# Spectral layer and two expert layers: four frequencies kept inside SBUF, and decode steps moved between stages

## The chip, the cores and the metric

The program runs on one core of a Trainium2 chip. The metric is the device time of one execution in microseconds; a median of several executions is compared. TensorE (PE) does the matmuls, VectorE (DVE) and ScalarE (ACT) do elementwise work, GpSimd (POOL) some of it, and SyncE (SP) issues most transfers.

## The reference

Three layers follow each other on 2 x 3008 tokens of width 256.

```python
X = np.fft.rfft(x, axis=1)                       # x: (2, 3008, 256)
Yr = Xr @ w_r - Xi @ w_i + b_r
Yi = Xr @ w_i + Xi @ w_r + b_i
Yr = np.sign(Yr) * np.maximum(np.abs(Yr) - 0.01, 0.0)    # Yi likewise
y = np.fft.irfft(Yr + 1j * Yi, n=3008, axis=1)
h = x @ w_in                                     # first expert: (6016, 256) @ (256, 2048)
x = (h - np.tanh(h)) @ w_out
h = x @ w_in2                                    # second expert
out = (h * np.clip(h + 3.0, 0.0, 6.0) / 6.0) @ w_out2
```

The experts' weights arrive as float64.

## The kernel before

**The spectral layer.** The transform of length 3008 = 47 x 64 is done in two steps. `dft_a` is the first step: it takes one of 16 chunks of x (eight of each batch row), multiplies it by `amt` and leaves 24 complex frequencies k for both parities on 96 partitions. `dft_a_out` evicts the two PSUM banks of a chunk on ScalarE, back into the chunk's own buffer (`xa` for the first batch, `xb` for the second), and stores it from ScalarE's queue to the DRAM array `s1`. `load_bi` reads four frequencies at a time back from `s1` into `bi_all`, now with 128 partitions in another order. `dft_b(j)` is the second step for two frequencies: four matmuls (L301), which need `bi_all` and the matching part of `bmt`. `evict_b_hi`, `_lo` and `_neg` split its result into a high part `fh` and a low part `fl`. `linear(j)` is the complex matrix product in 24 matmuls. `shrink`, `shrink_hi`, `shrink_lo` apply bias and threshold and split again (`sh`, `sl`). `dft_c` and `dft_d` are the two steps of the inverse transform, with a store to DRAM between them (`co`).

The frequency loop runs over t = 0 to 23. Iteration t does `linear(t)`, `dft_c(t-2)`, `dft_b(t+2)`, and, while chunks of the second batch are left, one `dft_a`. Every engine executes its instructions in the order in which the code is written.

**The decode.** `w_steps` is a generator that turns one float64 weight chunk of 512 KB (`raw`) into high and low float32 parts. Each call of `w_step` emits its next piece: on ScalarE L172 and L173 or the rounding copy L182, on VectorE L175, L185, L190, L197, or a pair of L201 to L205. Five calls decode a chunk of an output matrix and seven a chunk of an input matrix, with four and eight VectorE instructions. One of the pieces issues the next load of a `raw` buffer; there are three. `ptr["dec"]` counts decoded chunks; the first expert has 16, and the loop decodes up to `NDEC` = 13 of them, four calls in each iteration from t = 2 on.

**The experts.** Tokens come in eight blocks of 752; a pass k = 0 to 7 takes one block through the first expert, a pass 8 to 15 one through the second. Each pass has eight groups g of hidden units. A group is seven products in PSUM banks `al`, `be` and `ga` (a fast 2 x 2 matrix scheme), the nonlinearity (`e`, `g`, `c`, `su`, `s`), its split (`gh`, `gl`), and the output matmuls. `first_group` is the first group of pass 0; its pieces stand between the last iterations' `dft_c`. `super_hook` is called at the positions a to e of each group and adds what is due there: operands of the next block, and decode steps. In pass 0 it calls `w_step` at all five positions of groups 1 to 7, in the later ones of the first expert at b, c and d of groups 1 to 5.

**Transfers.** The transfers of SyncE and ScalarE share eight semaphores (DMAHW0 to 7) in rotation. A transfer that reuses one is issued only when the one before it on that semaphore has landed.

The lines that the prediction names: L269 `dft_a`, L279 its eviction, L280 its store, L290 `load_bi`, L301 `dft_b`, L308 the high part `fh`, L315 the low part `fl`, L407 a difference of operands, L418 the high half of an operand, L538 the first eviction of `first_group`, L575, L587 and L596 evictions and sums of a group.

Of the kernel before, what the change touches and what calls it, by code (L numbers as in the profile page):

```python
# [10 lines left out]
F32 = mybir.dt.float32  # L11
# [9 lines left out]
K1 = 24  # L21
D = 256
# [5 lines left out]
def dft_constants():  # L28
# [44 lines left out]

    am96 = np.zeros((96, 96))
    am96[0:94] = am.reshape(94, 96)
    cm = cm.reshape(128, K1 * 128).astype(f)
# [11 lines left out]
def spectral_moe_kernel(ctx: ExitStack, tc: tile.TileContext, x, w_r, w_i, b_r, b_i,  # L88
# [48 lines left out]

    NDEC, NST = 13, 2
    w_src = {"1i": w1i, "1o": w1o, "2i": w2i, "2o": w2o}
# [72 lines left out]
    def w_step():  # L212
        next(w_gen, None)
# [20 lines left out]
    bias = ca.tile([128, 1, D], F32, name="bias")  # L234
    amt = ca.tile([96, 96], F32, name="amt")
    x1 = [wia.tile([128, 4, D], F32, tag=f"wo{5 + r}", name=f"xb{r}") for r in range(3)]
# [3 lines left out]
    wa = wa_cm.__enter__()  # L240
    x0 = [wa.tile([128, 4, D], F32, name=f"xa{r}") for r in range(8)]
    stores = []

    def load_x(i):
        if i >= 16:
            return
        b, c = divmod(i, 8)
        if b == 0:
            v = x.rearrange("b s d -> (b s) d")[0:96 * 32].rearrange("(r j) d -> r j d", j=32)
            sp.dma_start(out=x0[c][0:96], in_=v[:, 4 * c:4 * c + 4, :])  # L250
        else:
            v = x[b].rearrange("(r j) d -> r j d", j=32)[:, 4 * c:4 * c + 4, :]
            for r0, r1 in ((0, 80), (80, 94)):
                sp.dma_start(out=x1[c % 3][r0:r1], in_=v[r0:r1])
# [6 lines left out]
    def dft_a(i, finish=True):  # L261
        b, c = divmod(i, 8)
        xt = (x1[c % 3] if b else x0[c])[0:96]
        banks_ = []
        for g in range(2):
            p = bank("acc" if i < 8 and i % 2 else "h")
            pv = p[0:96].rearrange("p (u d) -> p u d", d=D)
            for u in range(2):
                pe.matmul(out=pv[:, u, :], lhsT=amt, rhs=xt[:, 2 * g + u, :], start=True, stop=True)  # L269
            banks_.append(pv)  # L270
        if finish:
            dft_a_out(i, banks_)
        return banks_

    def dft_a_out(i, banks_):
        b, c = divmod(i, 8)
        xt = (x1[c % 3] if b else x0[c])[0:96]
        for g in range(2):
            act.activation(out=xt[:, 2 * g:2 * g + 2, :], in_=banks_[g], func=ACTF.Copy)  # L279
        act.dma_start(out=s1w[b][:, 4 * c:4 * c + 4, :], in_=xt)  # L280

# [3 lines left out]
    def load_bi(i):  # L285
        if i >= 2 * K1 // GB:
            return
        b, g = divmod(i, K1 // GB)
        t = bi_ring[i % 3]
        sp.dma_start(out=t, in_=s1[b][g * GB:(g + 1) * GB].rearrange("k p d -> p k d"))  # L290
        bi_t[i] = t
# [316 lines left out]
    with tc.manual_schedule():  # L608
# [13 lines left out]
        for i in range(8):  # L622
            load_x(i)
        for r in range(3):
            pool.memset(x1[r][64:96], 0.0)
# [6 lines left out]
        load_bm(0)  # L632
        sp.dma_start(out=dmt, in_=dm)
        for k, w in enumerate((b_r, b_i)):
            sp.dma_start(out=bias[64 * k:64 * k + 64, 0, :],
                         in_=w.rearrange("(o d) -> o d", o=1).broadcast_to([64, D]))
        for i in range(8):
            dft_a(i)
        load_x(8)
        load_bi(0)  # L640
        load_x(9)
        load_bi(1)
        load_bm(1)
        load_cm(0, x0[7][0:1, 3, 0:1])
        load_x(10)
        w_load()
        wa_cm.__exit__(None, None, None)
        wpool["r"] = ctx.enter_context(tc.tile_pool(name="wr", bufs=1, side="right", reuse_waits="tile"))
        for k in range(2):
            split(lwH[:, k], lwL[:, k], lws[k])  # L650
        for j in range(2):
            dft_b(j)
            evict_b_hi(j)
            evict_b_lo(j)
            evict_b_neg(j)
        load_bi(2)
        NP = K1
        a_next = 8
        for t in range(NP):
# [10 lines left out]
            shrink(t)  # L670
            shrink_hi(t)
            if t + 2 < NP:
                evict_b_lo(t + 2)
            if t == NP - 1:
                first = first_group()
                next(first)
            if t + 2 < NP:
                evict_b_neg(t + 2)
            for _ in range(2):
                if t > 1 and ptr["dec"] < NDEC:  # L680
                    w_step()
# [11 lines left out]
            if t % 2 == 0:  # L693
                load_bm(t // 2 + 2)
                load_cm(t // 2 + 1, s_t[t][0].bitcast(F32)[0:1, 0, 0:1])
            if t > 0:
                load_x(10 + t)
            if t in (0, 1):
                w_load()
            if t % 2 == 1:  # L700
                load_bi((t + 1) // 2 + 2)
            for _ in range(NST):
                if t > 1 and ptr["dec"] < NDEC:
                    w_step()
# [10 lines left out]
            if t == 22:  # L715
                op_sub(T3, B22, B12)
                op_sub(T4, B21, T2)

# [14 lines left out]
        def super_hook(k, g, pos):  # L733
# [12 lines left out]
            if n < 2 * NS:  # L746
# [21 lines left out]
                if g == 7 and pos == "e":  # L768
                    op_split(n, "b22")
            if 1 <= g < 6 or k == 0 and g > 0:  # L770
                if (pos in "bcd" or k == 0) and k < NS:
                    w_step()
            if pos == "e" and k in (NS - 1, NS):
# [54 lines left out]
```

## Time and profile before

| | us |
|---|---|
| median of 3 runs (lowest, highest) | 1226.78 (1226.3, 1228.44) |
| profiled execution | 1225.78 |
| its span, first to last instruction | 1224.0 |
| TensorE busy | 1183.5 |
| VectorE busy | 962.5 |
| ScalarE busy | 880.8 |

The profile is of one execution. What lies between span and time is start and end of the program. Busy times overlap; a stage is read from its own rows. Where the granted clock of TensorE has no record yet, at the start, the column shows 1.00.

### The profile page before, as it was taken

To read this page: it belongs to the slowest core of one execution; us is meant where nothing else is said; L and a number is where in the kernel's file an instruction comes from. 1 tells how busy PE (TensorE), PEld (TensorE's weight loads), DVE (VectorE), ACT (ScalarE), POOL (GpSimd) and SP (SyncE) were. 2 spreads that over 40 slices of the span, in tenths; PEclk is the share of its full clock that TensorE was granted. 3 is DMA by queue.
4 is the path that set the end of the run, shared out by engine and by line. 5 is a ranking of instruction groups with operands and counts; after the bars stand their busy time and mean duration, and the time that the engine had idled before them with its cause. 6 is when DMAs were issued, how large, how long until landed. Compare 5 with 4: busy or idle time off the path is not lost.

```text
span 1224.0 us, 20880 instructions
## 1 busy us (share of the span) xinstructions
PE 1183.5 (97%) x7824; PEld 1163.0 (95%) x7824; DVE 962.5 (79%) x1808; ACT 880.8 (72%) x1836; POOL 158.7 (13%) x164
## 2 busy tenths in 40 slices
PE   5899979899999999999999999999999999999998
PEld 3799969899999999999999999999999999999998
DVE  0479988888888888888778787878787878787875
ACT  3477767777787777777777777777777777777775
POOL 1000010201102020202021320202020202020200
PEclk9899989999999999999999999999999999999999
DMA  9896522232212122211104530101010101001000
GB/s 269 239 334 209 185 86 67 99 106 74 74 49 98 66 69 69 61 60 44 43 1 166 185 130 1 51 1 52 1 52 1 52 1 35 18 22 31 10 18 26
DMA packets 47797, 96.51 MB, mean 79 GB/s; under 512 B 4448, under 2 KB 27488, under 8 KB 47696
## 3 DMA queue, kind: packets, MB, share of 16 engines
q1 hardware_dynamic: 41728, 74.08, 18.8%
q0 software_dynamic: 4032, 14.68, 3.9%
q10 hardware_dynamic: 1936, 6.42, 1.4%
q8 instruction: 61, 1.00, 0.3%
q14 instruction: 40, 0.33, 0.1%
HBM read 58.73 MB, written 36.44 MB: 78 GB/s over the span
## 4 chain that ended last, share of the span: by engine, by line
PE 76%; DVE 10%; ACT 10%; issue 3%; DMA 2%; SPq 0%; ACTq 0%; DVEq 0%
PE acc L119 13%; PE acc L121 13%; PE acc L120 13%; PE al L119 7%; PE al L120 6%; PE al L121 6%; PE be L121 3%; PE be L120 3%; PE be L119 3%; ACT gh L115 2%; DVE g L440 2%; PE ga L398 2%; PE ga L120 2%; PE ga L121 2%; PE ga L119 1%
## 5 line engine op out<-in xcount | busy, mean ns | idle before, releaser
L116 DVE TENSOR_TENSOR gl<-g,gh 128x376 fp32r<-128x376 f32 x509 | 290.4, 571 | 149.7 <-ACT gh L115 122.1
L115 ACT ACTIVATE gh<-g 128x376 fp32r<-128x376 f32 x509 | 263.5, 518 | 185.5 <-DVE g L443 91.8
L121 PE MATMUL acc<-wo,gl 128*128 128x256 f32 (+1 forms) x768 | 215.9, 281 | 0.0
L120 PE MATMUL acc<-wo,gh 128*128 128x256 f32 (+1 forms) x768 | 215.8, 281 | 0.0
L119 PE MATMUL acc<-wo,gh 128*128 128x256 f32 (+1 forms) x768 | 215.7, 281 | 0.0
L119 PE MATMUL acc<-gh,wo 128*128 128x376 f32 x512 | 173.2, 338 | 0.0
L121 PE MATMUL acc<-gh,wo 128*128 128x376 f32 x512 | 171.0, 334 | 0.0
L120 PE MATMUL acc<-gl,wo 128*128 128x376 f32 x512 | 170.7, 333 | 0.0
L120 PEld LDWEIGHTS acc<-wo,gh 128*128 128x128 f32 (+1 forms) x768 | 143.0, 186 | 0.0
L121 PEld LDWEIGHTS acc<-wo,gl 128*128 128x128 f32 (+1 forms) x768 | 143.0, 186 | 0.0
L119 PEld LDWEIGHTS acc<-wo,gh 128*128 128x128 f32 (+1 forms) x768 | 142.8, 186 | 0.0
L407 POOL TENSOR_TENSOR bmt<-bmt 128x376 f32<-128x376 f32 x62 | 73.9, 1192 | 521.5 <-ACT bmt L400 396.8
L443 DVE SCALAR_TENSOR_TENSOR g<-e,c 128x376 f32<-128x376 f32 x192 | 119.3, 621 | 12.5 <-ACT e L442 7.9
L442 ACT ACTIVATE e<-c,three 128x376 f32<-128x376 f32 x192 | 116.7, 608 | 8.0 <-DVE c L589 7.2
L440 DVE TENSOR_TENSOR g<-c,e 128x376 f32<-128x376 f32 x189 | 113.9, 603 | 8.2 <-ACT e L439 6.0
L423 POOL TENSOR_TENSOR cmL<-bmt,cmH 128x376 fp32r<-128x376 f32 x60 | 66.1, 1102 | 325.8 <-ACT cmH L418 322.5
L439 ACT ACTIVATE e<-c 128x376 f32<-128x376 f32 x189 | 97.5, 516 | 7.9 <-DVE c L589 7.7
L119 PEld LDWEIGHTS acc<-gh,wo 128*128 128x128 f32 x512 | 96.4, 188 | 0.0
L120 PEld LDWEIGHTS acc<-gl,wo 128*128 128x128 f32 x512 | 96.3, 188 | 0.0
L121 PEld LDWEIGHTS acc<-gh,wo 128*128 128x128 f32 x512 | 96.1, 188 | 0.0
L119 PE MATMUL al<-cmH,wi 128*128 128x376 f32 x256 | 87.8, 343 | 6.3 <-ACT bi_all L538 2.9
L579 ACT ACTIVATE s<-be 128x376 f32<-128x376 f32 x127 | 61.9, 487 | 39.8 <-PE be L121 39.4
(164 smaller groups left out, 2830.8 us busy)
## 6 DMA issues: line engine op xcount, KB each, us to landing
raw<-in_moe_w_in_dram SPq DMA_DIRECT2D x16, 512.0 KB, 5.0
raw<-in_moe_w_out_dram SPq DMA_DIRECT2D x16, 512.0 KB, 4.4
w2id<-wout SPq DMA_DIRECT2D x8, 896.0 KB, 4.3
wi<-w2id POOLq DMA_DIRECT2D x8, 896.0 KB, 4.9
bi_all<-s SPq DMA_DIRECT2D x12, 512.0 KB, 6.5
y1d<-y SPq DMA_DIRECT2D x32, 188.0 KB, 2.0
bmt<-y1d SPq DMA_DIRECT2D x8, 752.0 KB, 4.9
s<-co SPq DMA_DIRECT2D x23, 256.0 KB, 5.5
```

The source lines that it names most:

```text
L115: act.activation(out=hi, in_=src, func=ACTF.Copy)
L116: (lo_eng or dve).tensor_tensor(out=lo, in0=src, in1=hi.bitcast(F32), op=ALU.subtract)
L119: pe.matmul(out=out_ap, lhsT=lh, rhs=rh, start=start, stop=False, **kw)
L120: pe.matmul(out=out_ap, lhsT=lh, rhs=rl, start=False, stop=False, **kw)
L121: pe.matmul(out=out_ap, lhsT=ll, rhs=rh, start=False, stop=stop, **kw)
L407: eng.tensor_tensor(out=out, in0=a, in1=b, op=ALU.subtract)
L423: (eng or dve).tensor_tensor(out=l, in0=OPS[nm][0], in1=h.bitcast(F32), op=ALU.subtract)
L439: act.activation(out=e, in_=src, func=ACTF.Tanh)
L440: dve.tensor_tensor(out=g, in0=src, in1=e, op=ALU.subtract)
L442: act.activation(out=e, in_=src, func=ACTF.Relu, bias=three)
L443: dve.scalar_tensor_tensor(out=g, in0=e, scalar=6.0, in1=src, op0=ALU.min, op1=ALU.mult)
L579: act.activation(out=s5, in_=be, func=ACTF.Copy)
```

## The change

`am` gets 32 more columns, copies of those of frequencies 0 to 7, so that `dft_a` of the first batch leaves them on partitions 96 to 127 as well. The eight buffers `xa` become one tile. After chunk 7, four transfers from `xa` to `bi_all` replace the first `load_bi`. ScalarE and VectorE evict one bank each for the first nine chunks. The ninth chunk is transformed ahead of the loop. Four matmuls on zeros stand ahead of everything on TensorE.

The decode starts ahead of the loop with five calls. An iteration makes six calls up to t = 9 and three or four from t = 10 on. In pass 0 there are four calls in groups 1 to 5 until 16 chunks are decoded, and none in groups 6 and 7; in later passes position a of groups 1, 3 and 5 is added. Two differences of operands (T3, T4) go from GpSimd to VectorE, and the last `shrink_hi` stands behind the first part of `first_group`.

```diff
-    am96 = np.zeros((96, 96))
-    am96[0:94] = am.reshape(94, 96)
+    am96 = np.zeros((96, 128))
+    am96[0:94, 0:96] = am.reshape(94, 96)
+    am96[0:94, 96:128] = am.reshape(94, K1, 4)[:, 0:8].transpose(0, 2, 1).reshape(94, 32)
...
-    x0 = [wa.tile([128, 4, D], F32, name=f"xa{r}") for r in range(8)]
+    xa = wa.tile([128, 32, D], F32, name="xa")
+    x0 = [xa[:, 4 * r:4 * r + 4, :] for r in range(8)]
...
         for g in range(2):
-            act.activation(out=xt[:, 2 * g:2 * g + 2, :], in_=banks_[g], func=ACTF.Copy)
-        act.dma_start(out=s1w[b][:, 4 * c:4 * c + 4, :], in_=xt)
+            if g and i < A0:
+                dve.tensor_copy(out=xt[:, 2 * g:2 * g + 2, :], in_=banks_[g])
+            else:
+                act.activation(out=xt[:, 2 * g:2 * g + 2, :], in_=banks_[g], func=ACTF.Copy)
+        act.dma_start(out=s1w[b][:, 4 * c:4 * c + 4, :], in_=xt[0:96])
...
+        warm = ca.tile([128, 256], F32, name="warm")
+        dve.memset(warm, 0.0)
+        for _ in range(4):
+            p = bank("h")
+            pe.matmul(out=p[:, 0:256], lhsT=warm[:, 0:128], rhs=warm, start=True, stop=True)
...
-        for i in range(8):
+        for i in range(A0):
             dft_a(i)
-        load_x(8)
-        load_bi(0)
+            if i == 5:
+                for k in range(2):
+                    split(lwH[:, k], lwL[:, k], lws[k])
+            if i == 7:
+                for k in range(GB):
+                    sp.dma_start(out=bi_ring[0][:, k, :], in_=xa[96 + k:128:8])
+                bi_t[0] = bi_ring[0]
...
+        for _ in range(5):
+            w_step()
...
-            shrink_hi(t)
+            if t < NP - 1:
+                shrink_hi(t)
...
                 first = first_group()
                 next(first)
+                shrink_hi(t)
...
-            for _ in range(2):
+            for _ in range(3 if t < 10 else 2):
...
-            for _ in range(NST):
+            for _ in range(3 if t < 10 else 1 + t % 2):
...
-                op_sub(T3, B22, B12)
-                op_sub(T4, B21, T2)
+                op_sub(T3, B22, B12, dve)
+                op_sub(T4, B21, T2, dve)
...
-            if 1 <= g < 6 or k == 0 and g > 0:
-                if (pos in "bcd" or k == 0) and k < NS:
-                    w_step()
+            if 1 <= g < 6 and k < NS:
+                if pos in "bcd" or pos == "a" and (k == 0 or g % 2):
+                    if k or ptr["dec"] < 16:
+                        w_step()
```

SyncE, behind the loads of x and of the linear weights: the queue up to the first frequencies, before (with the semaphores that a row waits for).

```order
L613 DMA bmt<-in_bm_dram 128x512 [waits DMAHW6_49]
L633 DMA dmt<-in_dm_dram 96x94 [waits DMAHW7_49]
L635 DMA bias<-in_b_r_dram 64x256 [waits DMAHW0_49]
L635 DMA bias<-in_b_i_dram 64x256 [waits DMAHW2_49]
L254 DMA xb_98<-in_x_dram 80x1024 [waits DMAHW3_49,Pool_49]
L254 DMA xb_98<-in_x_dram 14x1024 [waits DMAHW4_49]
L290 DMA bi_all<-s_0_60 128x4x256 [waits DMAHW6_49,DMAHW5_49,DMAHW7_49,DMAHW1_49,DMAHW0_49]
```

The same place after the change.

```order
L620 DMA bmt<-in_bm_dram 128x512 [waits DMAHW7_49]
L257 DMA xb_98<-in_x_dram 80x1024 [waits DMAHW1_49,Pool_49]
L257 DMA xb_98<-in_x_dram 14x1024 [waits DMAHW2_49]
L158 DMA raw<-in_moe_w_in_dram 128x2x256 [waits DMAHW4_49]
L648 DMA bias<-in_b_r_dram 64x256 [waits DMAHW5_49]
L648 DMA bias<-in_b_i_dram 64x256 [waits DMAHW6_49]
L657 DMA bi_all<-xa 128x1x256 [waits DMAHW1_49,DVE_49,Activation_49]
L657 DMA bi_all<-xa 128x1x256 [waits DMAHW2_49]
L657 DMA bi_all<-xa 128x1x256 [waits DMAHW3_49]
L657 DMA bi_all<-xa 128x1x256 [waits DMAHW4_49]
```

The reload that waited for the stores is gone, a weight chunk stands ahead of the four copies, and the fourth copy waits for DMAHW4, which that weight chunk used last.

VectorE in iteration 21 of the frequency loop, before (L342 to L344 `shrink`, L354 `shrink_lo`, `ws` and `raw` decode).

```order
L342 TENSOR_TENSOR ly<-acc,bias 128x512
L343 TENSOR_SCALAR lc<-ly 128x512
L344 TENSOR_TENSOR ly<-ly,lc 128x512
L315 TENSOR_TENSOR fl<-ga,fh 128x4x128
L204 TENSOR_TENSOR ws<-ws 128x128
L205 TENSOR_TENSOR ws<-ws 128x128
L354 TENSOR_TENSOR sl<-ly,sh 128x512
L423 TENSOR_TENSOR cmL<-bmt,cmH 128x376
L407 TENSOR_TENSOR bmt<-bmt 128x376
L175 TENSOR_SCALAR raw<-raw 128x512
L185 SCALAR_TENSOR_TENSOR ws<-ws,raw 128x512
```

The same iteration after the change.

```order
L349 TENSOR_TENSOR ly<-acc,bias 128x512
L350 TENSOR_SCALAR lc<-ly 128x512
L351 TENSOR_TENSOR ly<-ly,lc 128x512
L322 TENSOR_TENSOR fl<-ga,fh 128x4x128
L361 TENSOR_TENSOR sl<-ly,sh 128x512
L430 TENSOR_TENSOR cmL<-bmt,cmH 128x376
L414 TENSOR_TENSOR bmt<-bmt 128x376
```

The four decode instructions are gone from the iteration; the rest stands in the same order.

VectorE in group 6 of the experts' first pass, before.

```order
L577 TENSOR_TENSOR c_2507<-ga,s_2505 128x376
L116 TENSOR_TENSOR gl<-g,gh 128x376
L440 TENSOR_TENSOR g<-c_2507,e 128x376
L201 TENSOR_TENSOR ws<-ws 128x128
L202 TENSOR_TENSOR ws<-ws 128x128
L589 TENSOR_TENSOR c_2537<-be,su 128x376
L116 TENSOR_TENSOR gl<-g,gh 128x376
L204 TENSOR_TENSOR ws<-ws 128x128
L205 TENSOR_TENSOR ws<-ws 128x128
L440 TENSOR_TENSOR g<-c_2537,e 128x376
```

The same group after the change.

```order
L584 TENSOR_TENSOR c_2496<-ga,s_2494 128x376
L117 TENSOR_TENSOR gl<-g,gh 128x376
L447 TENSOR_TENSOR g<-c_2496,e 128x376
L596 TENSOR_TENSOR c_2524<-be,su 128x376
L117 TENSOR_TENSOR gl<-g,gh 128x376
L447 TENSOR_TENSOR g<-c_2524,e 128x376
```

The decode pieces between the sums and the splits are gone; they stand in earlier iterations and in later passes.

## Rows read from the trace of the kernel before

**Rows 1.** The page: busy time and share of each engine.

```profile
PE 1183.5 (97%) x7824; PEld 1163.0 (95%) x7824; DVE 962.5 (79%) x1808; ACT 880.8 (72%) x1836; POOL 158.7 (13%) x164
```

**Rows 2.** Waits of TensorE, whole run: us in total, times, longest.

```profile
PE al L301 <- issue: 13.1, 1, 13.1
...
PE al L119 <- ACT bi_all L538: 2.9, 1, 2.9
PE al L119 <- DVE c L596: 2.9, 2, 2.3
PE acc L121 <- DVE fl L315: 2.0, 2, 1.5
PE al L119 <- ACT su L587: 2.0, 3, 0.9
PE acc L119 <- ACT fh L308: 1.8, 1, 1.8
PE al L119 <- ACT s L575: 1.7, 3, 0.8
```

**Rows 3.** Timeline of the head: start, us, engine, line, operation, [idle before, releaser].

```profile
5.71 1.99 PE L269 MATMUL al<-xa,amt 96*96 96x256 f32 x4 [5.71 <-DMA xa<-in_x_dram]
...
11.96 1.03 PE L269 MATMUL al<-xa,amt 96*96 96x256 f32 x4
...
19.58 0.59 ACT L279 ACTIVATE xa<-al 96x512 f32<-96x512 f32 x1 [3.37 <-DMA lwf<-in_w_i_dram]
...
20.59 1.89 PE L269 MATMUL acc<-xa,amt 96*96 96x256 f32 x8
...
25.25 0.31 ACTq L280 DMA_DIRECT2D s<-xa  x1
...
28.76 0.40 SPq L290 DMA_DIRECT2D bi_all<-s  x1
...
35.54 2.05 PE L301 MATMUL al<-bmt,bi_all 128*128 128x128 f32 x8 [13.05 <-issue]
37.38 1.63 PE L301 MATMUL be<-bmt,bi_all 128*128 128x128 f32 x8
...
42.08 1.06 PE L301 MATMUL al<-bmt,bi_all 128*128 128x128 f32 x8
```

**Rows 4.** Windows in the head: engines' busy time, clock, DMA share, last column GB/s.

```profile
18.00:20.00 2.00, 2.00 (x11) 1.52 (x10) 0.00 (x0) 0.42 (x1) 0.00 (x0) 1.00 1.00 390
...
40.00:42.00 2.00, 2.00 (x19) 2.00 (x19) 0.69 (x1) 0.85 (x3) 0.00 (x0) 1.00 1.07 365
```

**Rows 5.** The loop: a window (third pair is VectorE), timeline rows of `dft_b`.

```profile
105.00:125.00 20.00, 19.90 (x171) 19.66 (x169) 19.62 (x37) 14.91 (x31) 0.00 (x0) 1.00 0.52 170
...
85.85 1.05 PE L301 MATMUL ga<-bmt,bi_all 128*128 128x128 f32 x8
92.02 1.05 PE L301 MATMUL al<-bmt,bi_all 128*128 128x128 f32 x8
96.46 1.05 PE L301 MATMUL ga<-bmt,bi_all 128*128 128x128 f32 x8
```

**Rows 6.** Timeline, ScalarE at the end of the loop.

```profile
160.04 0.52 ACT L418 ACTIVATE cmH<-bmt 128x376 fp32r<-128x376 f32 x1 [2.82 <-DVE bmt L407]
```

**Rows 7.** Windows at the handover and in pass 0; last but two is the clock.

```profile
165.00:185.00 20.00, 16.00 (x81) 14.69 (x80) 16.32 (x30) 12.38 (x28) 2.06 (x2) 0.83 0.28 82
245.00:265.00 20.00, 18.54 (x99) 18.55 (x100) 17.92 (x38) 15.52 (x35) 1.79 (x2) 0.91 0.28 88
```

**Rows 8.** Timeline, L575 (once a group): starts of groups 6 and next 0, passes 0 and 2.

```profile
226.28 0.48 ACT L575 ACTIVATE s<-al 128x376 f32<-128x376 f32 x1
...
250.09 0.48 ACT L575 ACTIVATE s<-al 128x376 f32<-128x376 f32 x1
...
365.63 0.48 ACT L575 ACTIVATE s<-al 128x376 f32<-128x376 f32 x1
...
382.45 0.47 ACT L575 ACTIVATE s<-al 128x376 f32<-128x376 f32 x1
```

More of the change, by code (lines that the diff above doesn't have):

```diff
@@ L136, in alloc_w @@
         return W[nm, c]
-    NDEC, NST = 13, 2
+    A0 = 9
+    NDEC = 13
     w_src = {"1i": w1i, "1o": w1o, "2i": w2i, "2o": w2o}
@@ L234, in spectral_moe_kernel @@
     bias = ca.tile([128, 1, D], F32, name="bias")
-    amt = ca.tile([96, 96], F32, name="amt")
+    amt = ca.tile([96, 128], F32, name="amt")
     x1 = [wia.tile([128, 4, D], F32, tag=f"wo{5 + r}", name=f"xb{r}") for r in range(3)]
@@ L263, in dft_a @@
         xt = (x1[c % 3] if b else x0[c])[0:96]
+        m = 96 if b else 128
         banks_ = []
@@ L266, in dft_a @@
             p = bank("acc" if i < 8 and i % 2 else "h")
-            pv = p[0:96].rearrange("p (u d) -> p u d", d=D)
+            pv = p[0:m].rearrange("p (u d) -> p u d", d=D)
             for u in range(2):
-                pe.matmul(out=pv[:, u, :], lhsT=amt, rhs=xt[:, 2 * g + u, :], start=True, stop=True)
+                pe.matmul(out=pv[:, u, :], lhsT=amt[:, 0:m], rhs=xt[:, 2 * g + u, :], start=True, stop=True)
             banks_.append(pv)
@@ L276, in dft_a_out @@
         b, c = divmod(i, 8)
-        xt = (x1[c % 3] if b else x0[c])[0:96]
+        xt = x1[c % 3][0:96] if b else x0[c]
         for g in range(2):
-            act.activation(out=xt[:, 2 * g:2 * g + 2, :], in_=banks_[g], func=ACTF.Copy)
-        act.dma_start(out=s1w[b][:, 4 * c:4 * c + 4, :], in_=xt)
+            if g and i < A0:
[3 more added lines that the diff above has]
+        act.dma_start(out=s1w[b][:, 4 * c:4 * c + 4, :], in_=xt[0:96])
     bi_t, xf_t, s_t = {}, {}, {}
@@ L632, in spectral_moe_kernel @@
         load_bm(0)
-        sp.dma_start(out=dmt, in_=dm)
+        load_x(8)
+        w_load()
         for k, w in enumerate((b_r, b_i)):
@@ L643, in spectral_moe_kernel @@
         load_bm(1)
-        load_cm(0, x0[7][0:1, 3, 0:1])
         load_x(10)
         w_load()
+        sp.dma_start(out=dmt, in_=dm)
+        for _ in range(5):
+            w_step()
         wa_cm.__exit__(None, None, None)
         wpool["r"] = ctx.enter_context(tc.tile_pool(name="wr", bufs=1, side="right", reuse_waits="tile"))
-        for k in range(2):
-            split(lwH[:, k], lwL[:, k], lws[k])
         for j in range(2):
@@ L655, in spectral_moe_kernel @@
             evict_b_neg(j)
+            if j == 0:
+                load_cm(0, xf_t[0][0].bitcast(F32)[0:1, 0, 64:65])
         load_bi(2)
         NP = K1
-        a_next = 8
+        a_next = A0
         for t in range(NP):
@@ L695, in spectral_moe_kernel @@
                 load_cm(t // 2 + 1, s_t[t][0].bitcast(F32)[0:1, 0, 0:1])
-            if t > 0:
-                load_x(10 + t)
-            if t in (0, 1):
+            load_x(11 + t)
+            if t == 0:
                 w_load()
```

## The prediction

> **What bounds the kernel now.** I first read the shares of busy time: TensorE is busy for 1183.5 us of 1224.0 [rows 1]. So no engine but TensorE can set the end over most of the program, and only time in which it waits or runs at the lower clock can be won: 40.5 us of idle time and what the clock costs. Next, the list of what TensorE waited for [rows 2] says where that time lies. The reader should see three places. The head: 13.1 us before the first second-step transform (L301, `dft_b`). The end of the frequency loop: 1.8 us for `fh`, most of the 2.0 us for `fl`, 2.9 us for L538. The experts' first pass: 2.9, 2.0 and 1.7 us for `c`, `su` and `s`, 6.6 us together. No later line has a wait worth a row.
>
> The timeline of the head shows the chain behind the 13.1 us [rows 3]. TensorE ends chunk 7 at 20.59 + 1.89 = 22.5. ScalarE has lost 3.37 us ahead of its work on chunk 4, and issues the store of chunk 7 only at 25.25. SyncE waits for the stores until 28.76, and the reloaded frequencies are there at 35.54: 6.8 us for 512 KB. From there to the first `dft_b` inside the loop, at 42.08, it takes 6.5 us.
>
> **The head.** The change copies frequencies 0 to 3 from `xa` to `bi_all` inside SBUF. The wait for the stores (28.76 - 25.25 = 3.5 us) leaves this chain. ScalarE evicts one half of a chunk and VectorE the other, so chunk 7 can be ready one eviction (0.59 us, the row at 19.58) after TensorE's 22.5, at 23.1. The warm-up matmuls could bring TensorE forward: its first 16 instructions stand 6.25 us apart in all (5.71 to 11.96), the next 40 take 8.63 us, 0.39 against 0.22 us each, which is the two levels of its clock. That is at most 2.8 us; I count none of it, since ScalarE, not TensorE, was late, and it still queues behind stores that wait for DMA semaphores, and now also behind the two splits of the linear weights.
>
> The copies bring a wait of their own. They reuse the semaphores of earlier transfers; the fourth waits for the 512 KB weight load `raw`, which is new in front of them. Ahead of it in SyncE's queue stand the second linear weight, `bm` and chunk 8. At 18 us I put 3.4 MB still to move (1.4 MB of this queue, five stores of 0.39 MB); at the 390 GB/s of that stretch [rows 4] they take 8.7 us, and `raw` is nearly the last of them: 26.5. Behind the waiting copy SyncE holds chunk 9, frequencies 4 to 7 and `bm` of the next four, which the `dft_b` at the loop's start needs.
>
> No row shows a copy within SBUF out of four partitions. Lower bound: 365 GB/s, the best rate of such 1 KB pieces [rows 4], 1.4 us. Upper bound: the reload's 6.8 us [rows 3]. I take the upper one, because the pieces come out of few rows and share the engines with the stores: 26.5 + 6.8 = 33.3. Two of the four copies suffice for the first `dft_b`, so the second starts at 33.3, and the loop's first one 42.08 - 37.4 = 4.7 us later (37.38 is its old start): 38.0. The next four frequencies, loaded behind it, I put at 38.5. Against 42.08 that wins 3.6 us; with the fast copy it would be about 36.5, or 5.6 us; at worst nothing.
>
> The Trainium skill, "DMA: Bandwidth & Descriptors", section "Why a DMA increments its semaphore by 16 and not by 1", speaks against this edit: a transfer issued from SyncE runs on the largest number of engines, at most 16, that divides the slowest dimension of both sides. Here that is 4 and 128, so four engines, and four copies put 128 KB on each of the same four. With one sixteenth of the 365 GB/s apiece, an estimate, they would take 5.7 us, and the sum would be 1 us lower than mine. No run here shows such a transfer yet.
>
> **The loop.** One first-step chunk is transformed in the head, under the wait for the copies, and not in the loop: an iteration with one is 92.02 - 85.85 = 6.17 us long, one without 96.46 - 92.02 = 4.44 [rows 5]. That wins 1.7 us.
>
> The decode steps move: five ahead of the loop, six instead of four in iterations 2 to 9, three or four from 10 on. Thirteen chunks need 81 steps, so they end in iteration 17 instead of 21. In its densest stretch VectorE runs 37 instructions in 19.6 us, 0.53 us each [rows 5]; an iteration has five of its own and, as twelve steps hold twelve VectorE instructions, one for each step. Before: 9 x 0.53 = 4.77 us against TensorE's 4.44, a lag that grows by 0.33 over 14 iterations to 4.6 us at the loop's end. After: 11 x 0.53 = 5.83 us, under the 6.17 while chunks are transformed (to iteration 6), but 1.4 us too much in iterations 7 to 9, 4.2 us; then 8.5 x 0.53 = 4.5, level. So the peak of the lag is as large as before, but in iterations 9 to 17, and from 18 on VectorE needs only 2.7 us of 4.44 and catches up. I charge 1 us for that peak. If an instruction costs 0.6 us instead, the lag doubles and 7 us show. The five early steps need `raw`, lie on ScalarE ahead of the first eviction, and end near 31, under the copies. A third more weight traffic, 170 KB in 6.17 us or 28 GB/s, fits under the 365 GB/s.
>
> **The end of the loop.** The old lag met the handover. ScalarE stood 2.82 us behind a difference that VectorE delivered late [rows 6], and the 1.8, 1.5 of the 2.0, and 2.9 us of [rows 2] followed; with the clock at 0.83 for 20 us another 3.4 us of full-speed time went [rows 7]. Together 9.6 us. After the change VectorE is not late in iterations 20 to 22, `shrink_hi` of the last iteration no longer stands ahead of the eviction (L538) that TensorE waited 2.9 us for, and the two GpSimd differences go to VectorE for 2 x 0.53 us. What is late next is the low half of the last frequencies and the one `al` bank of the first products. I take 8 us, with 5 and 10 as ends.
>
> **The first expert pass.** Its groups 6 and 7 run from 226.28 to 250.09, 23.8 us; the same two of the third pass from 365.63 to 382.45, 16.8 us [rows 8]. The difference of 7.0 us contains five decode steps in each group, and all of them go. All waits of the pass, 6.6 us, and 20 x 0.09 = 1.8 us of clock [rows 2, 7] make 8.4. Groups 1 to 5 keep four steps instead of five. I take 7.5; ends 4 and 8.4. The steps that leave it go to later passes, 18 each instead of 15, in groups that had three: some 15 steps of 0.53 us under a TensorE that does not wait there. I charge 0.5 us; if that cover fails, 4.
>
> **The sum.** -3.6 - 1.7 + 1.0 - 8.0 - 7.5 + 0.5 = -19.3 us. The profiled execution took 1225.78, so 1206.5; it lies 1.0 us under the median of the three runs, so on their scale 1207.5.
>
> **Rivals.** First, the head gives nothing, because the copies and what queues behind them still end at 42: 1207.5 + 3.6 = 1211. For it: the DMA queues are full there. Against it: one transfer and its wait are gone. Second, VectorE becomes the bound in iterations 2 to 17, at 0.6 us an instruction: 6 us more, 1213.5. Against it speaks the 0.53 of its densest stretch. Third, the waits of the end and of the first pass only move, to bank turnover and to groups 1 to 5, and half of 15.5 us stays: 1215. Against it: groups 6 and 7 of the third pass do without such waits. Fourth, the other sign: the four copies crawl. They would have to end 19 us later than I say, 26 us instead of 6.8 for 512 KB, 20 GB/s, a little less than one engine's sixteenth of the 365 GB/s [rows 4]. If all four shared one engine they would take 23 us and the gain be nearly gone, 1223; at 33 us, 1233. The reload's row makes that unlikely. The change does what it says in every part, except that the warm-up may buy nothing.
>
> **Chances.** Forecast 0.60 (1201 to 1213), no head gain 0.12, VectorE 0.10, waits moved 0.10, crawl 0.08, of which half ends between. The range 1199 to 1217 takes in the bounds of the likeliest case (-5.6, -10, -8.4 and no charge for the loop give 1201.6; I add 2.6 us for what I have not seen) and the first three rivals. About 0.2% can be told from no change: faster 0.92, same 0.04, slower 0.04.
>
> **What would show it.** Right: the first `dft_b` near 31 and the loop's first near 38.5; no wait for L538 and none over 1 us for `fh` or `fl` after iteration 18; no low clock between 160 and 185; groups 6 and 7 of the first pass near 17 us; VectorE's busy share near 1 in iterations 7 to 17. Wrong: `dft_b` still waiting for the copies after 42, TensorE waiting for `fl` in iterations 3 to 15 by more than 3 us, or waits for `su`, `c` and `s` that reappear in groups 1 to 5 or in later passes.

## The result, and the profile after

The changed kernel takes 1214.09 us (median of 4 runs, 1212.14 to 1216.64), the kernel before 1226.54 beside it (4 runs): ratio 0.9903, 95% interval 0.9886 to 0.9919. So it is faster by 12.4 us, where 19.3 were forecast. The profiled execution took 1212.14 us with a span of 1210.3, 13.6 and 13.7 us less than the profiled one of before. The stages below are read from these two traces and add up to the span's 13.7.

The page of the changed kernel, busy time of each engine:

```profile
PE 1185.4 (98%) x7832; PEld 1164.5 (96%) x7832; DVE 965.6 (80%) x1820; ACT 875.2 (72%) x1827; POOL 157.2 (13%) x162
```

TensorE's waits inside the loop up to iteration 16 (40 to 132 us), changed kernel:

```profile
PE acc L122 <- DVE fl L322: 2.0, 3, 1.5
PE al L308 <- issue: 2.0, 1, 2.0
PE al L308 <- ACT co L379: 0.9, 1, 0.9
PE al L308 <- DMA bmt<-in_bm_dram: 0.8, 1, 0.8
PE ga L273 <- DVE lc L350: 0.2, 1, 0.2
```

The large waits of [rows 2] are gone: nothing like L538, and `s`, `su` and `c` have 0.2 to 0.3 us each in the whole run. In their place the loop, which had 1.2 us of waits before, has 6. The timeline of the head, changed kernel (L308 is `dft_b` now, L657 the copies):

```profile
17.51 1.89 PE L273 MATMUL acc<-xa,amt 96*128 96x256 f32 x8
...
23.10 0.31 ACTq L287 DMA_DIRECT2D s<-xa  x1
...
23.43 4.15 SPq L657 DMA_DIRECT2D bi_all<-xa  x4
...
28.55 1.19 PE L308 MATMUL al<-bmt,bi_all 128*128 128x128 f32 x4 [1.53 <-issue]
...
34.29 1.22 PE L308 MATMUL ga<-bmt,bi_all 128*128 128x128 f32 x4 [1.40 <-DMA bi_all<-xa]
...
39.58 1.06 PE L308 MATMUL al<-bmt,bi_all 128*128 128x128 f32 x8
```

Chunk 7 leaves TensorE at 19.4 us and its store is issued at 23.10, against 25.25 in [rows 3]. The first `dft_b` comes 7 us earlier than in [rows 3], but half of the second one waits for the last copy until 34.29, so the loop starts 2.5 us earlier, at 39.58 against 42.08.

Windows of the changed kernel: all copies in flight, the loop's two parts, its end, and groups 6 and 7 of the first pass (third pair VectorE, then the clock, the DMA share and GB/s):

```profile
27.00:28.00 1.00, 0.02 (x1) 0.00 (x0) 0.69 (x1) 0.00 (x0) 0.00 (x0) 0.50 0.27 97
39.58:91.60 52.02, 48.06 (x356) 44.56 (x355) 42.07 (x75) 36.40 (x71) 5.43 (x12) 1.00 0.96 298
91.60:130.85 39.25, 37.20 (x304) 36.29 (x305) 36.14 (x67) 26.02 (x52) 1.35 (x3) 1.00 0.65 189
157.72:176.10 18.38, 16.67 (x115) 15.21 (x114) 15.37 (x30) 11.97 (x26) 1.00 (x1) 1.00 0.17 58
217.64:234.69 17.05, 17.05 (x101) 17.05 (x100) 13.38 (x24) 11.94 (x28) 6.83 (x6) 1.00 0.00 0
```

The granted clock is at 1.00 where [rows 7] had 0.83 and 0.91, and TensorE is busy for all of groups 6 and 7.

The loop in the timeline of the changed kernel: TensorE's `dft_b`, SyncE's queue, and a hand-over between ScalarE and VectorE.

```profile
78.24 1.13 PE L308 MATMUL al<-bmt,bi_all 128*128 128x128 f32 x8 [0.89 <-ACT co L379]
...
83.28 0.38 SPq L158 DMA_DIRECT2D raw<-in_moe_w_in_dram  x1
83.70 0.47 SPq L262 DMA_DIRECT2D s<-co  x1
84.22 0.56 SPq L620 DMA_DIRECT2D bmt<-in_bm_dram  x1
...
91.60 1.13 PE L308 MATMUL al<-bmt,bi_all 128*128 128x128 f32 x8 [2.04 <-issue]
...
105.07 1.06 PE L308 MATMUL be<-bmt,bi_all 128*128 128x128 f32 x8
...
107.34 0.63 ACT L357 ACTIVATE sh<-ly 128x512 fp32r<-128x512 f32 x1 [3.57 <-DVE ly L351]
...
107.90 0.39 PE L122 MATMUL acc<-lwH,fl 128*128 128x256 f32 x1 [1.53 <-DVE fl L322]
...
108.87 0.43 DVE L177 TENSOR_SCALAR raw<-raw 128x512 uint32<-128x512 uint32 x1 [1.03 <-ACT ws L174]
...
111.44 1.06 PE L308 MATMUL al<-bmt,bi_all 128*128 128x128 f32 x8
```

Two things are to be seen. At 83.28 SyncE's queue has stood at a weight load that waits for the decode step which frees its buffer (L187); the output store and `bm` queue behind it, and `bm` of the next frequencies, issued at 84.22, is what TensorE needs at 91.60. And iteration 11 (105.07 to 111.44) takes 6.37 us where 4.44 were enough before: ScalarE stands at `sh` until VectorE delivers `ly`, the next decode step's L174 lies behind it on ScalarE, and VectorE then waits 1.03 us for that.

### The profile page after: what moved, and what is told of

It reads as the page before. It is cut to its first block, busy times and chain, and to the rows that moved or that the text cites. A ratio compares the mean times of both kernels' runs of the same rounds, so it can differ in the third digit from the quotient of the medians.

```text
span 1210.3 us, 20904 instructions
## 1 busy us (share of the span) xinstructions
PE 1185.4 (98%) x7832; PEld 1164.5 (96%) x7832; DVE 965.6 (80%) x1820; ACT 875.2 (72%) x1827; POOL 157.2 (13%) x162
## 4 chain that ended last, share of the span: by engine, by line
PE 73%; DVE 11%; ACT 11%; DMA 2%; issue 2%; SPq 0%; ACTq 0%; DVEq 0%
PE acc L122 13%; PE acc L120 13%; PE acc L121 13%; PE al L120 6%; PE al L121 6%; PE al L122 6%; PE be L122 3%; PE be L121 3%; PE be L120 3%; ACT gh L116 3%; DVE g L447 3%; PE ga L405 2%; DVE gl L117 2%; PE ga L121 1%; PE ga L122 1%
## 5 line engine op out<-in xcount | busy, mean ns | idle before, releaser
L586 ACT ACTIVATE s<-be 128x376 f32<-128x376 f32 x127 | 61.8, 487 | 40.5 <-PE be L122 39.9
```

Of the source, the lines that this page charges most:

```text
L586: act.activation(out=s5, in_=be, func=ACTF.Copy)
```

## The experiments

All are edits of the changed kernel; e1 to e4, e5 to e8 and e9 to e12 each ran on one chip beside the kernel before, whose median was 1225.0, 1226.1 and 1225.9 us there (the row "before" is that of the changed kernel's run). The table gives the median (ratio to before and its interval) and the stages of the one profiled execution of each kernel in us: start of the loop's first `dft_b`, from there to iteration 8, on to 16, to 21, to the first `s` of the experts' first pass (the end of the loop), the rest of that pass, and the later passes. Without any wait the stages to 8 and to 16 would be 47.1 (5.49 + 6 x 6.19 + 4.46; before, with one chunk more, 1.7 longer) and 35.7 (8 x 4.46).

| kernel | median, ratio | start | to 8 | to 16 | to 21 | end | pass 0 | later |
|---|---|---|---|---|---|---|---|---|
| before | 1226.5 | 42.1 | 49.9 | 36.0 | 26.7 | 27.5 | 67.9 | 973.9 |
| changed | 1214.1, 0.9903 | 39.6 | 52.0 | 39.3 | 26.9 | 18.4 | 58.6 | 975.6 |
| e1 pace 4 | 1220.6, 0.9956 (0.9941-0.9970) | 40.1 | 53.0 | 38.6 | 27.5 | 24.4 | 60.1 | 975.9 |
| e2 late loads | 1214.3, 0.9908 (0.9893-0.9922) | 40.0 | 47.2 | 43.9 | 26.9 | 18.6 | 60.3 | 975.6 |
| e3 steps by room | 1215.5, 0.9916 (0.9903-0.9929) | 39.9 | 53.8 | 36.7 | 26.6 | 20.5 | 60.6 | 975.6 |
| e4 weight behind copies | 1219.3, 0.9945 (0.9930-0.9959) | 46.2 | 51.6 | 39.5 | 26.9 | 18.4 | 59.3 | 975.7 |
| e5 old reload | 1213.2, 0.9893 (0.9879-0.9906) | 39.8 | 52.6 | 40.0 | 26.9 | 18.6 | 60.3 | 975.6 |
| e6 late, by room, 15 | 1213.9, 0.9895 (0.9882-0.9909) | 40.7 | 47.3 | 39.9 | 26.7 | 20.9 | 59.4 | 975.9 |
| e7 late, 6/4, 15 | 1211.9, 0.9878 (0.9865-0.9891) | 41.9 | 47.6 | 39.5 | 25.9 | 19.1 | 59.2 | 975.2 |
| e8 old end, no warm-up | 1215.7, 0.9909 (0.9895-0.9922) | 41.6 | 51.7 | 39.6 | 26.9 | 19.7 | 58.5 | 975.5 |
| e9 late, no sums | 1209.6, 0.9867 (0.9850-0.9885) | 42.1 | 51.2 | 40.2 | 26.9 | 18.3 | 58.6 | 974.6 |
| e10 reload, late, 5/4 | 1212.5, 0.9895 (0.9879-0.9911) | 40.2 | 47.3 | 39.4 | 27.1 | 21.4 | 60.1 | 975.8 |
| e11 reload, late, 6/4 | 1209.5, 0.9868 (0.9853-0.9883) | 39.7 | 48.5 | 39.8 | 25.9 | 19.1 | 59.5 | 975.1 |
| e12 no shared eviction | 1214.5, 0.9909 (0.9893-0.9925) | 41.7 | 51.9 | 39.6 | 26.8 | 18.4 | 60.6 | 976.0 |

**e1, two plus two steps.**

```diff
-            for _ in range(3 if t < 10 else 2):
+            for _ in range(2):
...
-            for _ in range(3 if t < 10 else 1 + t % 2):
+            for _ in range(2):
```

> The changed kernel with two plus two decode steps in every iteration from t = 2 on (the pace of the kernel before); all else as changed. Theory: the loop is slower than forecast because six steps an iteration are more than VectorE and its hand-overs with ScalarE can do (12 steps and two times the five own instructions took 13.9 us in two iterations of the changed kernel, against 8.9 us of TensorE). Then the waits of the loop (L322 2.3 us, the second 'issue' 2.0, co 0.9) go, and the stretch from the loop's first dft_b to that of t = 21 falls from 118.1 us to about 112. The steps now end in iteration 20 or 21, so the lag meets the end of the loop again: of the 9.1 us won there some 4 are lost. Together about 1212 us. Rival 1: the gain at the loop's end came from shrink_hi and the two differences on VectorE and not from the steps: the end stays at 18.4 us, 1208. Rival 2: the loop is slow for another reason (fuller DMA queues, the copies): it stays near 118 and the time goes to 1218.

The end was as the theory says: with steps up to iteration 20 it takes 24.4 us and not 18.4, so 6 of the 9.1 us won there are the steps' leaving; rival 1 falls. The loop was not: 118.1 us became 119.1. In its first part one wait stayed (TensorE 1.9 us for `co`, whose store to `s` was late), and behind that wait TensorE ran at its lower level, 1.2 GHz; windows of e1 (the clock is the third number from the end):

```profile
77.00:80.00 3.00, 1.13 (x8) 0.97 (x8) 1.45 (x3) 0.81 (x2) 0.00 (x0) 0.97 1.05 339
80.00:84.00 4.00, 3.73 (x10) 2.67 (x11) 2.92 (x5) 3.21 (x7) 1.23 (x3) 0.50 1.05 377
84.00:90.00 6.00, 6.00 (x43) 6.00 (x43) 1.81 (x3) 2.12 (x4) 0.00 (x0) 0.78 0.68 208
```

These two iterations are 5.9 us longer than they are without a wait, and that is all that the first part has above its 47.1 us: the others run free at this pace. So the pace matters there, but the late store still came; the DMA share of 1.05 fits rival 2, fuller queues, and e2 decides between the two.

**e2, late weight loads.** `w_late` issues what the steps of the iteration before asked for.

```diff
-                w_load()
+                w_want()
...
                 load_bi((t + 1) // 2 + 2)
+            w_late()
```

> The changed kernel, but each weight load of the loop is issued an iteration later than the step that frees its buffer, behind the loads of bm and of the frequencies, so that SyncE no longer stands at a load that waits for VectorE (L187), with the output store, bm and the next frequencies behind it. Theory: part of the loop's loss is this queue (the load at 83.28 us waited for L187, bm behind it was issued at 84.22 and TensorE stood 2.04 us at 91.60; the store behind it made ScalarE wait 0.97 us for co). Then the waits of 2.04, 0.89 and 0.82 us go, the time falls by 3 to 4 us to about 1210.5; the waits for L322 stay. Rival: the DMA engines themselves are full (their share was above 0.9 for most of 40 to 90 us): waits move, time 1213 to 1215.

The waits of the first part went, all of them: 47.2 us, which is no wait at all, at a DMA share of 1.00. So that part had been lost to the order in SyncE's queue and not to full DMA engines. But the time stayed, because what was won up to iteration 8 was lost behind it. TensorE's waits of e2, 40 to 132 us:

```profile
PE acc L122 <- DVE fl L333: 3.8, 4, 1.5
PE acc L120 <- ACT fh L326: 1.4, 1, 1.4
```

From t = 0 to 16 it takes 91.1 us against 91.3. Neither theory had this: with the queue's stalls gone, a lag of VectorE and ScalarE that is as long shows in their place.

**e3, steps by room.**

```diff
-            for _ in range(3 if t < 10 else 2):
+            for _ in range(3 if t < 7 or t > 15 else 2):
...
-            for _ in range(3 if t < 10 else 1 + t % 2):
+            for _ in range(3 if t < 7 else 2 if t > 15 else 1 + t % 2):
```

> The changed kernel with the steps put where an iteration has room: six in t = 2 to 6 (6.2 us each), three or four in t = 7 to 15 (4.5 us each), five from 16 on (5.3 us each). Theory (VectorE): the 2.3 us for L322 in t = 11 to 16 and the longer iterations there go, loop 118.1 to about 114, the end of the loop keeps its gain: about 1210. Rival: what slows the loop starts in t = 2 to 6 (SyncE's queue behind the weight loads): the part up to t = 8, 52.0 us, stays, and of the later 66.1 us only 2 go: 1212.

Between: the second part is free of lag (36.7), the first stays at the queue (53.8), and the steps of iterations 16 to 18 cost the end 2.1 us. No gain in the time.

**e4, the first weight load behind the copies.**

```diff
         load_x(8)
-        w_load()
...
                 bi_t[0] = bi_ring[0]
+        w_load()
         load_x(9)
```

> The changed kernel with the first weight load issued behind the four copies, so that the fourth copy doesn't wait for it. Theory: the fourth copy (issued at 27.6, there at 34.3 us) is what TensorE waited for; it is issued 3 us earlier, the wait of 1.4 us before the second half of the second dft_b goes, and the loop's first dft_b moves from 39.6 to about 38.2 us: 1212.7. Rival: it is held by the traffic in the queues (stores and reloads) and lands no earlier, or the decode steps' late start takes it back: 1214.

Slower by 5 us, for a reason that neither had. ScalarE in the timeline of e4:

```profile
36.90 0.66 ACT L174 ACTIVATE ws<-raw 128x512 f32<-128x512 f32 x1 [10.01 <-DMA raw<-in_moe_w_in_dram]
...
38.03 0.58 ACT L315 ACTIVATE fh<-al 128x512 fp32r<-128x512 f32 x1
```

The early decode steps lie on ScalarE ahead of the first eviction `fh`, and wait 10 us for the weight. In the changed kernel that same L174 starts at 28.23 and is over in time: "under the copies" held, and this is what it costs where the weight is late. And the copies are not issued faster without the weight in front of them; SyncE in the timeline of e4:

```profile
24.36 3.73 SPq L656 DMA_DIRECT2D bi_all<-xa  x4
```

It is through with the last of them at 28.09, where the changed kernel, with the weight in front, is at 27.58. The last copy landed at 35.0, no earlier either, so the wait for `raw` was not what held it.

**e5, the old reload.**

```diff
-                for k in range(GB):
-                    sp.dma_start(out=bi_ring[0][:, k, :], in_=xa[96 + k:128:8])
-                bi_t[0] = bi_ring[0]
+                load_bi(0)
```

> The changed kernel with the old reload of the first four frequencies (one load of 512 KB from DRAM, behind the stores of all eight chunks) in place of the four copies inside SBUF; the shared eviction, the warm-up and the ninth chunk stay. Theory: the copies save the wait for the stores and nothing in the transfer; the last store is issued at 23.1 us and the stores of the kernel before took 3.5 us more to be waited for and the reload 6.8, so the reload would be there at 33.4 at the earliest against 34.3 with the copies: the head's gain then comes from the faster eviction, the loop's first dft_b stays within 1 us of 39.6, and the time within 1 us of 1214.1. Rival (as predicted): the wait for the stores comes back in full, 3 to 4 us, loop from 43, 1217.5.

The theory holds. SyncE and TensorE in the timeline of e5:

```profile
28.35 0.39 SPq L297 DMA_DIRECT2D bi_all<-s  x1
...
33.20 2.05 PE L308 MATMUL al<-bmt,bi_all 128*128 128x128 f32 x8 [4.98 <-issue]
35.04 1.92 PE L308 MATMUL ga<-bmt,bi_all 128*128 128x128 f32 x8
39.78 1.06 PE L308 MATMUL al<-bmt,bi_all 128*128 128x128 f32 x8
```

The reload is issued at 28.35, 4.6 us behind the last store, and everything is there at 33.2, with all four frequencies at once. The four copies are issued 5 us earlier and end a us later.

**e6 and e7, both limits of the loop.** e6 is e2 and e3 together, e7 is e2 with `3 if t < 7 else 2` in both places; both take `pos == "a" and k == 0` for the fourth step of a group, which makes 15 a later pass.

> The changed kernel with the late weight loads of e2, the steps of e3 and, in the experts' later passes, 15 steps a pass as before the change in place of 18. Theory: two limits follow each other in the loop, SyncE's queue up to t = 8 and VectorE from t = 8 to 16; either edit alone only hands the time to the other. Together the stretch from t = 0 to 8 is 47.2 us as in e2, that from 8 to 16 is 36.7 as in e3, against 91.3 together in the changed kernel: 7.4 us; the end loses the 2 us of e3; the passes two to five win back the 1.3 us by which they are longer than before the change. Together about 1207.5 us. Rival: VectorE is the limit from t = 2 on and the lag of the first part shows in the second: 41 us there, 1212.

> As the run with late loads and steps by room, but with six steps in iterations 2 to 6 and four in all later ones, so that the steps end in iteration 18 and not 19. Theory: VectorE enters iteration 7 with little lag, loses about 0.5 us an iteration to t = 15 (3.0 us of its own work and four steps of 0.51 us against 4.47), shows 1 to 2 us of waits for L322 or L315 in t = 12 to 16, and has caught up by t = 20: end at 18.4 us. About 1207. Rival: the lag shows from t = 9 on, 4 us, 1210.

Both gain 4 us from t = 0 to 16 (87.2 and 87.1), by the rival's account: the lag of iterations 2 to 6 shows behind 8. The 15 steps give 1.4 us back in the second to seventh pass of both, and the eighth, into which the last three decode instructions on VectorE now fall, is 1.6 us longer in e6 and 1.1 in e7: as good as nothing. e6's median is that of the changed kernel, e7's 2.2 us below it, with intervals that overlap.

**e8, the old end, and no warm-up.**

```diff
-            if t < NP - 1:
-                shrink_hi(t)
+            shrink_hi(t)
...
-                op_sub(T3, B22, B12, dve)
-                op_sub(T4, B21, T2, dve)
+                op_sub(T3, B22, B12)
+                op_sub(T4, B21, T2)
```

> Two edits in stages far apart, to be read by the stages: the changed kernel without the four warm-up matmuls, and with the end of the loop as before (the last shrink_hi ahead of the other eviction, the two differences on GpSimd). Theory for the end: most of the 9.1 us came from the steps that no longer run there; the old order costs the 2.9 us for the eviction and about 1 us for the slower differences: 18.4 becomes 21 to 22 us. Rival: the order did nothing by itself, 18.4. Theory for the head: TensorE starts at the lower clock, ends chunk 7 some 2 us later, and as VectorE now shares the evictions TensorE counts: loop's first dft_b 1 to 2 us later. Rival (as predicted): nothing, 39.6. Together about 1219 us.

The four warm-up matmuls are left out as well. The end is 1.3 us longer (TensorE waits 2.1 us for the late eviction): the theory, at half of its size or less. The loop starts at 41.6, but so does that of e7 (41.9), which has the warm-up. For the head this run tells nothing.

**e9, less VectorE work.** This is e2 without the four sums of each `w_in` chunk, so its weights, and with them its output, are not those of the layer.

```diff
-                dve.tensor_tensor(out=ws[:, 4, :], in0=ws[:, 0, :], in1=ws[:, 2, :], op=ALU.add)
-                dve.tensor_tensor(out=ws[:, 6, :], in0=ws[:, 1, :], in1=ws[:, 0, :], op=ALU.subtract)
                 yield
-                dve.tensor_tensor(out=ws[:, 5, :], in0=ws[:, 4, :], in1=ws[:, 1, :], op=ALU.subtract)
-                dve.tensor_tensor(out=ws[:, 7, :], in0=ws[:, 3, :], in1=ws[:, 5, :], op=ALU.subtract)
```

> The run with late weight loads (e2: six steps an iteration, SyncE out of the way), with the four small VectorE instructions of every w_in chunk (L203 to L207, 0.95 us a chunk) left out, so that the decoded weights lack their four sums. Some six such chunks fall into the loop: 5.7 us of VectorE work. Theory: VectorE's own work is the limit of iterations 2 to 15, so the stretch from t = 0 to 16, 91.1 us in e2, falls by most of that, to 86 or 87. Rival: the limit is the hand-over between ScalarE and VectorE (about 1 us every second iteration, L177 behind L174) or the DMA queues: the stretch falls by less than 2 us.

From t = 0 to 16 91.4 us: no gain, but not a clean answer. A third limit came in, the weights themselves; ScalarE in the timeline of e9:

```profile
77.42 0.67 ACT L185 ACTIVATE ws<-raw 128x512 f32<-128x512 f32 x1 [5.15 <-DMA raw<-in_moe_w_in_dram]
```

That load was issued at 68.32 and took 9 us; `bm`, issued a us behind it, was late too, and TensorE stood for it and then ran at 1.2 GHz from 81 to 84:

```profile
80.83 1.96 PE L315 MATMUL al<-bmt,bi_all 128*128 128x128 f32 x8 [2.08 <-DMA bmt<-in_bm_dram]
```

VectorE's waits for ScalarE at the hand-over (L188 here; 40 to 132 us) were as long as in e2 with all its work (5.2 us, 5 times):

```profile
DVE raw L188 <- ACT ws L185: 5.4, 6, 1.0
```

So leaving out VectorE work does not shorten the hand-over; what each is worth in the lag is read further down, from all kernels together.

**e10 and e11, versions.** Old reload and late loads, with `3 if t < 7 else 2` and `2` steps (e10) or `3 if t < 7 else 2` twice (e11).

> The old reload (as e5), late weight loads (as e2), five steps in iterations 2 to 6 and four from 7 on. Theory (VectorE): with five steps of 0.51 us and 3.0 us of own work an iteration of 6.19 us leaves no lag, so the four steps in 7 to 15 (0.6 us an iteration too much) build up at most 5 us and TensorE hardly waits: t = 0 to 16 in 84 to 85 us instead of 87.1 with six steps in 2 to 6 (e7); the steps end in iteration 19, the end takes 19 to 21 us. About 1209. Rival: four steps in 4.47 us is what is too much, whatever came before: 87 us, and the end is later as well, 1213.

> The old reload (as e5), late weight loads, six steps in iterations 2 to 6 and four from 7 on (the loop of e7), 18 steps a pass as changed. Theory: the reload costs nothing against the four copies, which moved at 97 GB/s while nothing else moved: loop start 39 to 40.5, and with the loop of e7 87 us to t = 16: within 1.5 us of e7, 1210.5 to 1212. Rival: with SyncE free in the loop the copies' earlier release shows: 2 us more than e7.

e10 keeps TensorE free up to iteration 11 and loses 3.7 us in 12 to 15 (39.4 against 35.7); the end is 3 us longer: its rival. e11 is the best of those that compute the whole layer, 1209.53 us (1209.04 to 1209.77). Each against the kernel before beside it, it is also ahead of the changed kernel, by little (its interval ends at 0.9883, the changed kernel's begins at 0.9886); the two did not run side by side. It lacks the copies. From e7, which has them and 15 steps a pass, it cannot be told apart.

**e12, ScalarE evicts alone.**

```diff
-            if g and i < A0:
-                dve.tensor_copy(out=xt[:, 2 * g:2 * g + 2, :], in_=banks_[g])
-            else:
-                act.activation(out=xt[:, 2 * g:2 * g + 2, :], in_=banks_[g], func=ACTF.Copy)
+            act.activation(out=xt[:, 2 * g:2 * g + 2, :], in_=banks_[g], func=ACTF.Copy)
```

> The changed kernel with both halves of a head's chunk evicted by ScalarE again (copies, ninth chunk and warm-up stay). Theory: the shared eviction is what won in the head; ScalarE alone needs 2 x 0.55 us and a store's 0.31 a chunk and the two splits of 1.15 and 0.58 us besides: the last store is issued at 25 us or later instead of 23.1 to 24.1, the copies end 1.5 to 2.5 us later, the loop's first dft_b at 42 and the time 1216.5. Rival: stores and copies wait for DMA semaphores anyway, loop start stays at 39.6 to 41.9, 1214.

The last store is issued at 24.70 and not 23.10, as the theory says (22.35 to 24.06 in the kernels e1 to e7), and the loop starts 2.1 us later, which lies inside the spread of the unchanged heads (39.6 to 41.9). The time is that of the changed kernel: the rival.

## Why the prediction was right in its sign and too large

Its terms against the stages of the two profiled executions, in us:

| term | forecast | measured |
|---|---|---|
| head | -3.6 | -2.5 |
| ninth chunk and lag of the loop (t = 0 to 21) | -1.7 + 1.0 = -0.7 | +5.5 (112.6 to 118.1) |
| end of the loop | -8.0 | -9.1 |
| first pass | -7.5 | -9.3 |
| later passes | +0.5 | +1.7 |
| sum | -19.3 | -13.7 |

**The step that failed is the 1.0 us charged for the loop.** The chunk's 1.7 us came, so the loop lost 7.2: 3.8 up to iteration 8, 3.2 from there to 16, and 0.2 behind it. The rows behind it, SyncE's waits from 20 to 140 us and VectorE's in iterations 2 to 15, of the changed kernel:

```profile
SPq L158 <- DVE ws L187: 59.2, 13, 7.1
...
DVE raw L177 <- ACT ws L174: 5.2, 5, 1.0
...
DVE fl L322 <- ACT fh L316: 1.1, 4, 0.6
```

Of the kernel before:

```profile
SPq L156 <- DVE ws L185: 48.0, 10, 6.8
...
DVE fl L315 <- ACT fh L309: 4.6, 6, 1.5
...
DVE raw L175 <- ACT ws L172: 1.7, 3, 1.0
```

The step had three faults. It took 0.53 us for every VectorE instruction: the five own ones take 3.0 us, 0.6 each, and six steps some 3.0, about 6.0 together where it had 5.83; that is the least of the three. It left out the waits of VectorE for ScalarE at L177, five of 1.0 us each, 5.2 us against 1.7 before. (The waits for `fh` fell by as much, but there VectorE is ahead and loses nothing.) And it put the decode's weight traffic down to bandwidth ("28 GB/s, fits"; six steps for four are a half more, not a third, the 28 is right), while SyncE's queue is what it goes through: SyncE stood 59 us at weight loads behind L187, with stores, `bm` and frequencies behind. The length of that wait is not its price: 48 us of it before cost TensorE next to nothing.

e2 shows the queue (52.0 to 47.2), e3 the lag (39.3 to 36.7), e6 and e7 that the two overlap, so that 4 us come back from both. What the lag is made of can be read from iteration 8 to 16, where TensorE without a wait needs 35.7 us: VectorE's busy time and its waits at the hand-over (L177) together are 34.6 + 0 before (36.0 us long), 33.1 + 2.1 in e3 (36.7), 34.9 + 3.1 in e1 (38.6), 36.1 + 2.1 in the changed kernel (39.3), 38.5 + 0 in e7 (39.5) and 40.6 + 2.1 in e2 (43.9). Where the sum is above 35.7 us, the stretch is as long as the sum and about a us more. So VectorE sets the pace there, with its own work and with the hand-over, and own work alone is enough for it (e7):

```profile
89.50:129.02 39.52, 37.64 (x306) 36.40 (x305) 38.52 (x74) 27.99 (x57) 1.29 (x3) 1.00 0.64 212
```

That VectorE's share would be near 1 was half right: 36.14 of 39.25 us, 0.92, and 0.96 before, so that sign tells little. The sign of a wrong loop, more than 3 us of waits for `fl`, did not appear (2.0 us): iterations grew longer by more than the waits that the list shows. The rival "VectorE becomes the bound", with 1213.5, came nearest to the time; it had the place, and lacked the queue, so its nearness is partly luck. That the pace of before does not restore the loop of before (e1) comes from one late store with the lower clock behind it, up to iteration 8, and from the 3.1 us at the hand-over after it, with VectorE's work as before. Why the hand-overs wait there is not explained: e1 has the same number of steps an iteration but starts five steps on, so each step falls on another place in the iteration; that this is the cause was not tried.

**The head.** The mechanism was partly wrong. The last of the four copies was issued, `raw` thus there, by 27.6 (26.5 forecast), the second `dft_b` came at 34.29 (33.3), the loop at 39.58 (38.5): each number within 1.1 us (only the first `dft_b` was further off, 28.55 for 31). Some of that is luck: chunk 7's store left at 23.10, as forecast, but TensorE was through with the chunk at 19.4 and not 22.5, and its eviction stood behind the splits of the linear weights. That the fourth copy is held by `raw`, from which the 26.5 comes, is not borne out (e4). And the gain was put down to the copies, which save the wait for the stores, and e5 shows that they win nothing over the reload. The row at 27 us points to why: with the copies alone in flight the DMA engines move 97 GB/s at a share of 0.27, where 390 GB/s move with the engines full [rows 4]. The Trainium skill, "DMA: Bandwidth & Descriptors", section "Why a DMA increments its semaphore by 16 and not by 1", says just that, four engines for a slowest dimension of 4, and the trace agrees: 97 is a quarter of 390. Some of the head's gain e12 may give to the shared eviction (without it the last store is issued 1.6 us later); in the whole time it doesn't show. Six kernels with an unchanged head start the loop between 39.6 and 41.9 (changed, e1 to e3, e6, e7), so no head term under 2.4 us can be told from single traces. That goes for the -2.5 itself: the six start at 40.4 in the mean, 1.7 us ahead of the one trace of before. Which edit of the head wins it stays open.

**The end of the loop** was right, its parts too: the steps at least 6.0 (e1), the order of the last eviction and the two differences 1.3 (e8). The other kernels bear the steps out, by how far ahead of the `dft_b` of iteration 21 VectorE starts its last decode instruction: 12.4 us (changed, e2) with an end of 18.4 and 18.6, 9.1 (e7, e11) with 19.1, 7.1 (e3, e6) with 20.5 and 20.9, 2.8 (e10) with 21.4, and 4.7 us behind it (e1) with 24.4. The sign "no low clock between 160 and 185" held in the profiled execution, and not in all: e2, e5 and e12, whose code is the same from there on, show 0.86, e4 0.93. Windows of the changed kernel and of e12:

```profile
160.00:185.00 25.00, 23.12 (x144) 21.18 (x143) 21.29 (x42) 17.45 (x39) 1.00 (x1) 1.00 0.26 83
...
160.00:185.00 25.00, 23.29 (x139) 21.93 (x138) 19.64 (x38) 16.18 (x35) 1.00 (x1) 0.86 0.28 85
```

**The first pass** was right in its groups 6 and 7 (17.05 us, near 17). On the whole it was 1.8 us short in the profiled execution, but that is within what the clock does: in those four the same pass takes 59.3 to 60.6 us, a gain of 7.3 to 8.6. Groups 1 to 5 gained as well, 2.5 us in the changed kernel's profile. **The later passes** cost 1.7 and not 0.5, and the moved steps are most of it: the third to sixth pass take 266.2 us against 264.1 before, and 264.6 in e6 and e7, which have 15 steps a pass and not 18. There the steps left undone come up in the eighth pass, which is longer by 1.6 and 1.1 us. So TensorE hides less of the moved steps than the forecast took, wherever they go; what the rest of the 1.7 us is stays open.

## What to carry to other kernels

Before work is put into a loop, add up for each iteration not only the engines' busy time but each in-order queue that the work passes: a load that waits for a buffer holds every load and store behind it, and a short step on a second engine can cost a wait at the hand-over (1.0 us each time here). Where two such limits overlap, removing one shows nothing in the time; compare stage times, not totals, and remove both; and take a stage from several executions, for its clock can differ from one to the next. A copy inside SBUF is not cheaper than a reload as such: look at how few partitions it comes from.

## What the runs showed of the hardware

The four warm-up matmuls (from 1.20 to 4.7 or 5.0 us) brought the first chunk to the higher level, 2.4 GHz, in only half of the executions: its first four matmuls took 1.10 to 1.14 us in six of the twelve profiled kernels that have them (changed, e1, e2, e4, e6, e12) and 2.04 or 2.05 in the others, as in e8 without any, though TensorE had been idle for less than 1.2 us in all of them. With the shared eviction, chunk 7's store left at 22.35 to 23.61 in those at the higher level and at 23.56 to 24.77 in the others and e8; at the loop's start no difference can be told from the spread. And one wait of 1.9 us inside the busy loop was followed by 4 us at 0.50 and 6 us at 0.78 (e1): 3.3 us of full-speed time (4 x 0.50 + 6 x 0.22), more than the wait itself. The wait of 2.08 us in e9 was followed by 3 us at 0.50, the one of 2.04 us in the changed kernel (before 91.60) by none below 1.00.
